# A chunked state-space scan feeding a GELU MLP on one core: weight quarters and B, C of unit 1 issued from ACT's queue

## The chip, the core and the metric

The kernel runs on one core of one Trainium2 chip. The core has five engines with an instruction queue each: PE (TensorE, matmul), DVE (VectorE), ACT (ScalarE), POOL (GpSimd) and SP (SyncE, which only issues transfers and waits). An engine works through its own queue in order; semaphores tell one engine that another, or a transfer, is done. The metric is the device time of one execution in microseconds (us), lower being better. Times in profile rows are counted from the start of the profiled span.

## The reference

Two stages follow each other. The first is a scan over 24 chunks of 32 positions for 4 batches and 8 heads; the second is an MLP over the 3072 resulting tokens.

```python
# x: 4 x 8 x 768 x 32, a: 4 x 8 x 768, B and C: 4 x 8 x 768 x 16, all float32
for c in range(nc):                      # chunks of 32
    cum = np.cumsum(log_a[chunk], -1)
    M = einsum('bhin,bhjn->bhij', Cc, Bc) * exp(cum_i - cum_j) * causal
    y = einsum('bhij,bhjd->bhid', M, xc) + einsum('bhin,bhnd->bhid', Cc, state) * exp(cum)
    state = exp(sum(la)) * state + sum_j(Bc_j * xc_j * exp(cum_last - cum_j))
t = y.transpose(0, 2, 1, 3).reshape(3072, 256)
h = t @ w_in                             # 256 x 2048
g = 0.5 * h * (1 + tanh(sqrt(2 / pi) * (h + 0.044715 * h**3)))
out = g @ w_out                          # 2048 x 256
```

## The kernel before

The kernel takes its own chunk length of 128 positions and treats two chunks (256 positions of one batch) as one unit, so there are 12 units, 0 to 11. For a unit the small loads are B and C (128 KB each, `load_bc`, line 163) and x (256 KB, `load_x`, line 171). The decays `a` are one load of 96 KB at the start (line 173). DVE scales B and C by decay factors (`f_mul`, line 338), PE or a transposing DMA turns them round (`f_T`, `f_XT`), DVE makes a masked copy `ce` (`f_F`; for unit 0 half of it is made on ACT, line 381), PE forms the Gram blocks `gb` (`f_G`), DVE masks them into `m` (`f_M`), PE adds up the result (`f_Y`) and ACT copies it as bf16 into `xm` (`f_yev`, line 250; for unit 0 DVE copies one half). The chain of states (`f_D`, `f_S`, `f_SP`) goes from chunk to chunk. The chunk decays `pend` come from one small matmul (`f_pp`), which in this kernel is written into bank GB[1], the bank of the Gram blocks.

The MLP works on the same 256 tokens as a unit: 8 pieces of four matmuls with `w_in` (`f_s1`, line 511), each followed by a GELU on ACT (`f_gelu`, line 519), and for each 128 tokens 16 matmuls with `w_out` (`f_s2`, line 528), an evacuation (`f_oev`) and a store. Both weights are 2 MB in float32, loaded in four quarters of 512 KB each (`load_wi`, line 242, and `load_wo`, line 246, into tiles `wf`) and cast to bf16 (`f_wi`, `f_wo`, lines 250 and 252).

The order of everything is planned by a list scheduler, `run_order` (line 33): each piece of work is a node with an engine, an estimated duration, a priority and dependencies, and the nodes are then emitted engine by engine in that order. In the plan all loads are one serial resource "DMA" in the order of the list `HEAD` (line 555). On the chip all of them except B of unit 0 are issued by SP, one after the other: a, C0, x0, wi0, C1, wi1, B1, x1, wi2, wi3, C2, wo0, B2, wo1, wo2, wo3, x2, C3, and so on (the digit is the unit or the quarter). PE runs matmuls without a use (line 788) in planned gaps of the first 20 us.

In the built program eight semaphores serve all loads of SP and ACT, given out in turn in program order; the issue of a load first waits for the landing of the load that had its semaphore before, eight loads earlier.

Of the kernel before, what the change touches and what calls it, by code (L numbers as in the profile page):

```python
# [109 lines left out]
def kernel(  # L110
# [10 lines left out]
    nc = tc.nc  # L121
# [13 lines left out]

    const = ctx.enter_context(tc.tile_pool(name="const", bufs=1))
    ldn = ctx.enter_context(tc.tile_pool(name="ldn", bufs=NP))
    wfp = ctx.enter_context(tc.tile_pool(name="wfp", bufs=6))
    ldx = ctx.enter_context(tc.tile_pool(name="ldx", bufs=NP))
    xpool = ctx.enter_context(tc.tile_pool(name="xpool", bufs=4))  # L140
    WB = 4
# [79 lines left out]
    rps = {}  # L221
# [17 lines left out]

    def load_wi(q):  # L240
        WF[("i", q)] = wfp.tile([128, 2, 512], FP32, name="wf")
        nc.sync.dma_start(out=WF[("i", q)], in_=wi[:, :, q * 512:(q + 1) * 512])  # L242

    def load_wo(q):
        WF[("o", q)] = wfp.tile([128, 4, d_model], FP32, name="wf")
        nc.sync.dma_start(out=WF[("o", q)], in_=wo[:, 4 * q:4 * q + 4])

    def copy(eng, o, i):
        if eng == "ACT":
# [6 lines left out]
    def f_wi(q, k0, k1, eng):  # L256
        copy(eng, w_in_sb[:, k0:k1, q * 512:(q + 1) * 512], WF[("i", q)][:, k0:k1])

    def f_wo(q, eng):
        copy(eng, w_out_sb[:, 4 * q:4 * q + 4], WF[("o", q)])  # L260


    def f_clip():
# [276 lines left out]
    def f_store(gc, q):  # L540
# [31 lines left out]
    def frees(n, *by, i=0):  # L572
        if n.alloc:
            n.frees[i] += list(by)


    nload = [0]
    T0 = 0.95

    def none():  # L580
        pass

    def load_act(dur, k, fn, *args):
        i = add("ACT", 0.55, fn, *args, nc.scalar, deps=[agate], prio=k[0])
        return load(dur, none, deps=[i])

    def load(dur, fn, *args, deps=(), alloc=()):
        nload[0] += 1
        return add("DMA", DF * dur, fn, *args, deps=deps, done=1.35, alloc=alloc, prio=nload[0])
# [6 lines left out]
    agate = add("ACT", 2.8, none, prio=-300)  # L596
    an = load(T0 + 0.3, none)
    an.done = 1.55
    bl[0, 1] = bl[0, 0] = load(2 * LB, none)

    def load_x_n(j):
        xl[j] = load_act(LX, AQ["x", j], load_x, j) if ("x", j) in AQ else load(LX, load_x, j, nc.sync)

    def load_b_n(j, i):
        a = ("bc"[i], j)
        bl[j, i] = load_act(LB, AQ[a], load_bc, j, i) if a in AQ else load(LB, load_bc, j, i, nc.sync)

    def load_w_n(k, q):
        (win_l, won_l)[k][q] = load((LI, LO)[k], (load_wi, load_wo)[k], q, alloc="wf")

    for kind, i in HEAD:
        {"x": load_x_n, "b": lambda j: load_b_n(j, 0), "c": lambda j: load_b_n(j, 1),
         "wi": lambda q: load_w_n(0, q), "wo": lambda q: load_w_n(1, q)}[kind](i)
    for j in range(T3, NP):
        load_b_n(j, 1)
        load_b_n(j, 0)
# [2 lines left out]
    for q in range(4):  # L619
        e = WENG[0][q].split("+")  # L620
        wi_n[q] = [add(f, wdur[f] / len(e) + 0.03 * (len(e) - 1), f_wi, q, k * 2 // len(e),
                       (k + 1) * 2 // len(e), f, deps=[win_l[q]], prio=-8 + q) for k, f in enumerate(e)]
        e = WENG[1][q]
        wo_n[q] = add(e, wdur[e], f_wo, q, e, deps=[won_l[q]], prio=20 + q)
        frees(win_l[q], *wi_n[q])
        frees(won_l[q], wo_n[q])


    cl = add("DVE", 0.55, f_clip, deps=[an], prio=-190)
# [9 lines left out]
    ppn = add("PE", 0.3, f_pp, deps=[pen, RT0], prio=-100)  # L639
    pendn = add("ACT", 0.22, f_pend, deps=[ppn], prio=-66)  # L640
    RTN = add("PE", 0.9, f_RTN, deps=[ppn], prio=RP, alloc="bk")
    rnn = [add("ACT", 0.28, f_rn, r, deps=[RTN], prio=5) for r in range(2)]
    frees(RTN, *rnn)
# [5 lines left out]
    for j in range(NP):  # L649
# [3 lines left out]
        if b and t == 0:  # L653
# [4 lines left out]
                     deps=[bl[j, i], *hold, pnn[b] if b else rlo if not i else rc1 if j else rc0, *gone(j)])  # L658
              for i in (1, 0)}
        bnn[j] = ml[0]  # L660
        if j == 0:
# [27 lines left out]
        xcn[j] = add("POOL", 0.66, f_castx, j, "POOL", deps=[xl[j], pgate, *gone(j)],  # L689
                     prio=10.0 * g0 - 10 if j else -96)  # L690
        u = j
        q = 10.0 * g0
        nd = kept(u)
        if u == 2:
            RTN.deps.append(Yn[1])
        if u <= MERGE:
            Gn[u] = add("PE", 0.37, f_G, u, prio=(-85, -50)[u] if u < 2 else q, deps=Fn[u] + Mn.get(u - 1, []))
# [28 lines left out]
        full = MERGE <= u < NP - 1  # L726
        Yn[u] = add("PE", 0.42 + 0.11 * sum(gc % CPB > 0 for gc in (g0, g0 + 1)) + (0.5 if full else 0.0),
# [26 lines left out]
    for g, (c0, n) in enumerate(GROUPS):  # L754
        per = 512 // (n * Q)
        for tt in range(n):
            gc = c0 + tt
            for q in range(4):
                need = [geln[(g, i)] for i in range(4 * n) if i * per <= 4 * q + 3]
                nd = add("PE", 0.437, f_s2, g, tt, q, deps=need[-1:] + [wo_n[q], prev],  # L760
                         prio=PB + 10 * c0 + 10 * n + 2.5 * (4 * tt + q) + 1.2, alloc="bk" if q == 0 else ())
                if q == 0:
                    first = nd
                prev = nd
# [5 lines left out]
            else:  # L770
                add("OUT", 0.05, f_store, gc, nc.sync, deps=[oevn[gc]], prio=gc)

    Dns[1].deps.append(gpn[(0, 3)])
    for n, u in later:
        n.deps.append(gpn[(u, 0)])

# [12 lines left out]
                                 start=True, stop=True)  # L789
        return fill  # L790

    pools = {"bk": 4, "gram": 1, "m": 2, "wf": 6}
    for t, fn in run_order(nodes, pools, idle=idle, wait=("DVE", "POOL")):
        fn()

# [29 lines left out]
```

## Time and profile before

| what | value |
|---|---|
| median of 3 runs | 118.8 us (118.76 to 119.0) |
| the profiled execution, its time | 119.01 us |
| its span, first to last instruction | 117.3 us |
| PE busy | 108.0 us (92%) |
| ACT, DVE, POOL busy | 72.1, 60.9, 31.0 us |
| granted PE clock | 1.000 |
| read from HBM, written | 10.58 MB, 3.15 MB |

Span and time of the profiled execution differ by 1.7 us of start and end outside the span. Busy PE is modelled from pipelined matmuls, so it says where PE had work, not that it worked at its peak. A row of the timeline gives the start, the duration, engine, line, operation, tiles and count of a run of equal instructions, and in brackets how long the engine sat idle before and what ended that. "SPq" and "ACTq" are the sequencers of these engines when they issue a transfer.

### The profile page before, as it was taken

The numbers are of one execution on the slowest core, as the hardware profiler recorded it, in microseconds if no ns is written. First come the engines' busy times: TensorE is split into PE (matmuls) and PEld (weight loads), VectorE is DVE, ScalarE is ACT, GpSimd is POOL, SyncE is SP. The second block draws the span as 40 slices with busy tenths as digits, with TensorE's granted clock in tenths as the row PEclk, the third lists the DMA queues.
The fourth block names the chain that finished last, engine by engine and source line by source line (L and its number), as shares of the span: only waits on it lengthen the run. The fifth ranks groups of instructions, "written<-read, shape, count | busy, mean of one in ns | idle before, by whom it ended". The sixth has DMA issues, their size and how long they took to land.

```text
span 117.3 us, 3834 instructions
## 1 busy us (share of the span) xinstructions
PE 108.0 (92%) x1638; PEld 91.7 (78%) x1638; DVE 60.9 (52%) x130; ACT 72.1 (61%) x156; POOL 31.0 (26%) x57
## 2 busy tenths in 40 slices
PE   5985767998999999999999999999999999999980
PEld 5863546787888888888888888888888888888860
DVE  2876685493687396671892943905708309000110
ACT  5063866773449559495685683783965866857610
POOL 6964364455332214103401303102111010000000
PEclk9999999999999999999999999999999999999999
DMA  3989999999979796499942962141101111011031
GB/s 74 209 245 221 263 253 293 347 169 184 222 150 157 128 229 164 75 225 188 144 78 56 215 164 62 45 50 45 50 0 45 50 38 52 6 45 48 0 98 45
DMA packets 46850, 15.04 MB, mean 128 GB/s; under 512 B 42320, under 2 KB 45232, under 8 KB 46832
## 3 DMA queue, kind: packets, MB, share of 16 engines
q1 hardware_dynamic: 44928, 12.29, 51.2%
q0 software_dynamic: 864, 2.36, 6.9%
q8 instruction: 13, 0.21, 0.8%
q10 hardware_dynamic: 1040, 0.13, 0.7%
q14 instruction: 5, 0.04, 0.1%
HBM read 10.58 MB, written 3.15 MB: 117 GB/s over the span
## 4 chain that ended last, share of the span: by engine, by line
PE 74%; DMA 11%; SPq 8%; POOL 2%; issue 1%; DVE 0%; DVEq 0%
PE bk L528 36%; PE bk L511 30%; DMA wf<-in_moe_w_out_dram 6%; DMA wf<-in_moe_w_in_dram 5%; SPq L242 5%; PE bk L434 3%; PE gb L399 3%; SPq L171 2%; PE bk L423 2%; PE bk L449 1%; SPq L163 1%; POOL w_out_sb L252 1%; POOL w_in_sb L252 1%; DVE o_sb L537 0%; SPq L173 0%
## 5 line engine op out<-in xcount | busy, mean ns | idle before, releaser
L519 ACT ACTIVATE gT<-bk 128x512 bf16<-128x512 f32 x96 | 50.6, 601 | 10.6 <-PE bk L511 10.6
L528 PE MATMUL bk<-w_out_sb,gT 128*128 128x256 bf16 x384 | 49.1, 273 | 0.9 <-POOL w_out_sb L252 0.5
L511 PE MATMUL bk<-xm,w_in_sb 128*128 128x256 bf16 x384 | 47.5, 273 | 1.2 <-POOL w_in_sb L252 1.1
L528 PEld LDWEIGHTS <-gT 128*128 128x128 bf16 x384 | 36.6, 98 | 7.4 <-issue 3.2
L511 PEld LDWEIGHTS <-w_in_sb 128*128 128x128 bf16 x384 | 37.2, 98 | 6.3 <-POOL w_in_sb L252 1.7
L409 DVE TENSOR_TENSOR m<-gb,tri 128x1024 bf16<-128x1024 f32 x23 | 27.8, 1217 | 1.7 <-PE gb L399 1.7
L542 POOL DMA_DIRECT2D out_dram<-o_sb x18 | 9.9, 551 | 42.5 <-ACT o_sb L535 40.6
L535 ACT ACTIVATE o_sb<-bk 128x256 f32<-128x256 f32 x22 | 8.5, 387 | 11.7 <-ACT xm L250 5.1
L477 DVE SCALAR_TENSOR_TENSOR s_new<-s_new,pend,bk 128x64 f32<-128x64 f32 x16 | 4.4, 275 | 19.1 <-ACT xm L250 18.4
L250 ACT ACTIVATE xm<-bk 128x256 bf16<-128x256 f32 x23 | 7.6, 380 | 9.5 <-PE bk L449 8.4
L338 DVE TENSOR_TENSOR bc<-bc,fac 128x256 bf16<-128x256 f32 x24 | 9.6, 430 | 5.6 <-DMA bc<-in_B_dram 3.3
L252 POOL CAST x<-x_t 128x512 bf16<-128x512 f32 x12 | 7.5, 629 | 12.1 <-DMA x_t<-in_x_dram 11.7
L493 DVE SCALAR_TENSOR_TENSOR sp_new<-s_new,pend,bmask 128x256 bf16<-128x256 f32 x19 | 9.6, 534 | 0.1
L537 DVE COPY o_sb<-bk 128x256 f32<-128x256 f32 x2 | 0.8, 424 | 14.0 <-PE bk L528 14.0
L383 DVE TENSOR_SCALAR ce<-bt,par 128x256 bf16<-128x256 bf16 x22 | 5.9, 318 | 2.8 <-ACT bt L250 1.7
L788 PE MATMUL bk<-wz 128*128 128x128 bf16 x66 | 6.2, 261 | 1.3 <-DVE warm L180 1.3
L788 PEld LDWEIGHTS <-wz 128*128 128x128 bf16 x66 | 5.2, 121 | 1.6 <-DVE warm L180 1.2
L434 PE MATMUL bk<-m,x 64*32 64x128 bf16 x384 | 5.2, 219 | 0.7 <-DVE m L409 0.7
L252 POOL CAST w_out_sb<-wf 128x1024 bf16<-128x1024 f32 x4 | 4.2, 1040 | 4.8 <-DMA wf<-in_moe_w_out_dram 4.8
L399 PE MATMUL gb<-ce,bt 32*64 32x256 bf16 x192 | 5.3, 280 | 0.1
L252 POOL CAST w_in_sb<-wf 128x1024 bf16<-128x1024 f32 (+1 forms) x4 | 3.7, 932 | 4.4 <-DMA wf<-in_moe_w_in_dram 4.4
L475 DVE COPY s_new<-bk 128x64 f32<-128x64 f32 x3 | 0.7, 224 | 7.5 <-ACT xm L250 7.5
(61 smaller groups left out, 45.7 us busy)
## 6 DMA issues: line engine op xcount, KB each, us to landing
x_t<-in_x_dram SPq DMA_DIRECT2D x12, 256.0 KB, 4.6
out_dram<-o_sb POOLq DMA_DIRECT2D x18, 128.0 KB, 3.0
wf<-in_moe_w_in_dram SPq DMA_DIRECT2D x4, 512.0 KB, 6.1
wf<-in_moe_w_out_dram SPq DMA_DIRECT2D x4, 512.0 KB, 7.5
bc<-in_C_dram SPq DMA_DIRECT2D x12, 128.0 KB, 4.5
bc<-in_B_dram SPq DMA_DIRECT2D x11, 128.0 KB, 4.2
out_dram<-o_sb SPq DMA_DIRECT2D x6, 128.0 KB, 1.7
bc<-in_B_dram ACTq DMA_DIRECT2D x1, 128.0 KB, 3.1
```

Of the source, the lines that this page charges most:

```text
L252: nc.gpsimd.tensor_copy(out=o, in_=i)
L338: nc.vector.tensor_tensor(out=d["bc16"][:, i], in0=d["bc"][:, i].rearrange("p h (r n) -> p r h n", r=2), in1=f.rearrange("p r (h o) -> p r ...
L399: nc.tensor.matmul(out=GB[g // 2][ks, g % 2, 256 * r:256 * r + 256], lhsT=d["bt"][gs, 0, r, ks], rhs=ce[gs, :, :, ks], start=True, stop=Tr ...
L409: nc.vector.tensor_tensor(out=state[("m", u, f)].rearrange("p g r e t -> p g (r e t)"), in0=state.pop(("gc", u, f), gram[f]).rearrange("p ...
L434: nc.tensor.matmul(out=y[k][32 * q:32 * q + 32, w * Q:(w + 1) * Q], lhsT=X16[u][ks, r, 32 * h:32 * h + 32], rhs=m[w][ks, q // 2, r, q % 2, :],
L493: nc.vector.scalar_tensor_tensor(out=sp_new.rearrange("p (g d) -> p g d", g=4), in0=state[("s", gc)].rearrange("p (o d) -> p o d", o=1).to ...
L511: nc.tensor.matmul(out=hp[:, j * nt:(j + 1) * nt], lhsT=w_in_sb[:, kc, fi * 128:(fi + 1) * 128], rhs=xm[:, kc, c0 * Q:c0 * Q + nt], start= ...
L519: nc.scalar.activation(gts[g][:, i * per:(i + 1) * per, 0:nt], hps.pop((g, i)).rearrange("p (j t) -> p j t", j=per), AF.Gelu_apprx_tanh)
L528: nc.tensor.matmul(out=ops[gc], lhsT=gts[g][:, fi, tt * Q:(tt + 1) * Q], rhs=w_out_sb[:, fi, :], start=(fi == 0), stop=(fi == NF - 1), ski ...
L535: nc.scalar.activation(o_sb, ops.pop(gc), AF.Copy)
L542: q.dma_start(out=out[u * W:(u + 1) * W].rearrange("(p r) m -> r p m", r=2)[r], in_=ops.pop(gc))
L788: nc.tensor.matmul(out=BK[j][:, 0:128], lhsT=wz[:, 0:128], rhs=wz[:, 0:128], start=True, stop=True)
```

## The change

ACT's queue now issues B0 (as before), C1, B1 and all eight weight quarters; SP keeps a, C0, x0, x1, C2, B2, x2, C3, B3, x3 and the rest. The tiles `wf` go from 6 buffers to 8. `f_pp` gets a bank of its own from the pool of four. The cast of wi0 is split in two halves on POOL, its half on ACT for wi1 goes to POOL, and the casts of wo2 and wo3 are split between POOL and DVE. Unit 2's transposed copy is made on DVE in place of ACT. D and G of unit 3 stand by themselves (`MERGE` 3). The planner gets new durations, a limit on outstanding descriptors (`RING`), a second load resource "DW" for the weights, priorities `WP` for the weight issues on ACT and two dependencies for them (wi2 after `f_rlo`, wo0 after the copy `s0`).

```diff
-    wfp = ctx.enter_context(tc.tile_pool(name="wfp", bufs=6))
+    wfp = ctx.enter_context(tc.tile_pool(name="wfp", bufs=8))
...
     load_bc(0, 0, nc.scalar)
     load_bc(0, 1, nc.sync)
+    load_bc(1, 1, nc.scalar)
+    load_bc(1, 0, nc.scalar)
...
-        nc.sync.dma_start(out=WF[("i", q)], in_=wi[:, :, q * 512:(q + 1) * 512])
+        nc.scalar.dma_start(out=WF[("i", q)], in_=wi[:, :, q * 512:(q + 1) * 512])
...
-        nc.sync.dma_start(out=WF[("o", q)], in_=wo[:, 4 * q:4 * q + 4])
+        nc.scalar.dma_start(out=WF[("o", q)], in_=wo[:, 4 * q:4 * q + 4])
...
-    def f_wo(q, eng):
-        copy(eng, w_out_sb[:, 4 * q:4 * q + 4], WF[("o", q)])
+    def f_wo(q, k0, k1, eng):
+        copy(eng, w_out_sb[:, 4 * q + 2 * k0:4 * q + 2 * k1], WF[("o", q)][:, 2 * k0:2 * k1])
...
-    def f_pp():
-        rps["pp"] = GB[1][:, 0, 0:NCH]
+    def f_pp(bk):
+        rps["pp"] = bk[:, 0:NCH]
...
+    WP = (-185, -184.9, -179.5, -179.4, -64, -63, -59, -58)
...
-    MERGE = 2
+    MERGE = 3
...
-    DF = 1.07
+    DF = 1.0
+    RING = 212
...
-    PET = {0: "ACT", 1: "ACT", 2: "ACT", 3: "ACT"}
-    LB, LX, LI, LO, XD, XL = 0.85, 1.15, 1.6, 1.5, 0.6, 3.6
-    HEAD = [("x", 0), ("wi", 0), ("c", 1), ("wi", 1), ("b", 1), ("x", 1), ("wi", 2), ("wi", 3),
-            ("c", 2), ("wo", 0), ("b", 2), ("wo", 1), ("wo", 2), ("wo", 3), ("x", 2)]
-    WENG = [("POOL", "POOL+ACT", "POOL", "POOL"), ("POOL", "POOL", "POOL", "POOL")]
+    PET = {0: "ACT", 1: "ACT", 2: "DVE", 3: "ACT"}
+    LB, LX, LI, LO, XD, XL = 0.92, 1.25, 1.85, 1.65, 0.6, 3.6
+    HEAD = [("x", 0, 2.6), ("x", 1, 3.0), ("c", 2, 5.5), ("b", 2, 3.7), ("x", 2, 2.3)]
+    SIDE = [*(("wi", q, 1.6, WP[q]) for q in range(4)), *(("wo", q, 1.75, WP[4 + q]) for q in range(4))]
+    WENG = [("POOL+POOL", "POOL", "POOL", "POOL"), ("POOL", "POOL", "POOL+DVE", "POOL+DVE")]
...
-    RP = 2000
+    RP = 4
+    XP = {0: -96, 1: -9}
+    D1 = None
+    WD = 0
...
+    was, issue = agate, {}
+    for i, dur in ((1, 5.0), (0, 1.6)):
+        bl[1, i] = add("DW", dur, none, done=1.35, prio=-i)
+    for k, (kind, i, dur, prio) in enumerate(SIDE):
+        was = issue[kind, i] = add("ACT", 0.5, load_wi if kind == "wi" else load_wo, i, deps=[was],
+                                   prio=prio)
+        lat = add(f"L{k}", 1.1, none, deps=[was])
+        n = add("DW", dur, none, deps=[lat], done=1.35, prio=k)
+        (win_l, won_l)[kind == "wo"][i] = n
...
+    issue["wi", 2].deps.append(rlo)
...
+                if WD is not None:
+                    issue["wo", WD].deps.append(sn)
...
-    Dns[1].deps.append(gpn[(0, 3)])
+    if D1 is not None:
+        Dns[1].deps.append(gpn[(0, D1)])
```

In the built program ACT's queue begins as follows. The names are those of the loads above; behind an issue stands the landing for which it waits because of the semaphores given out in turn, two queues now sharing the eight. The planner has no node for these waits.

| ACT's queue in order | waits for |
|---|---|
| issue B0, C1, B1 | nothing |
| load of the function table, `warm` | DVE's `warm` |
| issue wi0 | nothing |
| issue wi1 | landing of C0 |
| `fac` (`f_rlo`) | DVE |
| issue wi2 | landing of wi0 |
| issue wi3 | landing of B2 |
| `ce` of unit 0, `bt`, `pend`, `gs`, `s0`, `s_new` | PE, DVE |
| issue wo0 | landing of x3 |
| issue wo1 | landing of wi2 |
| issue wo2 | landing of C4 |
| issue wo3 | landing of wi3 |
| `xm` of unit 0, `bt` of unit 1, GELUs of group 0 | PE, DVE |

SP's queue is a, C0, x0, x1, C2 (waits for B0), B2 (a), x2 (C1), C3 (x0), B3 (B1), x3 (x1), C4 (C2), B4 (wi1), x4 (x2), C5 (C3), B5 (B3), and then the first transposing DMA.

More of the change, by code (lines that the diff above doesn't have):

```diff
@@ L577, with load @@
     nload = [0]
-    T0 = 0.95
+    T0 = 1.05
     def none():
         pass
[L583 to L587, printed above, removed]
+    ring = []
+    def load(dur, fn, *args, deps=(), alloc=(), desc=65):
         nload[0] += 1
-        return add("DMA", DF * dur, fn, *args, deps=deps, done=1.35, alloc=alloc, prio=nload[0])
+        cum = (ring[-1][1] if ring else 0) + desc
+        full = [m for m, c in ring if cum - c <= RING]
+        room = [add(f"R{nload[0]}", 1.1, none, deps=full[:1])] if cum > RING and full else []
+        n = add("DMA", DF * dur, fn, *args, deps=[*deps, *room], done=1.35, alloc=alloc, prio=nload[0])
+        ring.append((n, cum))
+        return n
     win_l, won_l, wi_n, wo_n = {}, {}, {}, {}
@@ L594, with load_x_n, load_b_n @@
     Gn, Mn, Yn, yevn, Sn, SPn, Fn, bnn, gcn, Dns = ({} for _ in range(10))
-    agate = add("ACT", 2.8, none, prio=-300)
-    an = load(T0 + 0.3, none)
+    agate = add("ACT", 3.8, none, prio=-300)
+    an = load(T0 + 0.3, none, desc=7)
     an.done = 1.55
     bl[0, 1] = bl[0, 0] = load(2 * LB, none)
[L601 to L613, printed above, removed]
+    def load_x_n(j, dur=None):
+        xl[j] = load(dur or LX, load_x, j, nc.sync)
+    def load_b_n(j, i, dur=None):
+        bl[j, i] = load(dur or LB, load_bc, j, i, nc.sync)
+    for kind, i, dur in HEAD:
+        if kind == "x":
+            load_x_n(i, dur)
+        else:
+            load_b_n(i, "bc".index(kind), dur)
+    was, issue = agate, {}
[7 more added lines that the diff above has]
+        (win_l, won_l)[kind == "wo"][i] = n
     for j in range(T3, NP):
@@ L622 @@
                        (k + 1) * 2 // len(e), f, deps=[win_l[q]], prio=-8 + q) for k, f in enumerate(e)]
[L623 to L626, printed above, removed]
+        e = WENG[1][q].split("+")
+        wo_n[q] = [add(f, wdur[f] / len(e) + 0.03 * (len(e) - 1), f_wo, q, k * 2 // len(e),
+                       (k + 1) * 2 // len(e), f, deps=[won_l[q]], prio=20 + q) for k, f in enumerate(e)]
     cl = add("DVE", 0.55, f_clip, deps=[an], prio=-190)
@@ L637 @@
     rlo = add("ACT", 0.2, f_rlo, deps=[RT0, rc0], prio=-180)
+    issue["wi", 2].deps.append(rlo)
     rc1 = add("DVE", 0.36, f_rc1, deps=[rc0, rlo], prio=-62)
-    ppn = add("PE", 0.3, f_pp, deps=[pen, RT0], prio=-100)
+    ppn = add("PE", 0.3, f_pp, deps=[pen, RT0], prio=-100, alloc="bk")
     pendn = add("ACT", 0.22, f_pend, deps=[ppn], prio=-66)
+    frees(ppn, pendn)
     RTN = add("PE", 0.9, f_RTN, deps=[ppn], prio=RP, alloc="bk")
@@ L660 @@
         bnn[j] = ml[0]
+        if j == 1:
+            ml[1].deps.append(Mn[0][1])
+            ml[0].deps.append(Mn[0][1])
         if j == 0:
@@ L689 @@
         xcn[j] = add("POOL", 0.66, f_castx, j, "POOL", deps=[xl[j], pgate, *gone(j)],
-                     prio=10.0 * g0 - 10 if j else -96)
+                     prio=XP.get(j, 10.0 * g0 - 10))
         u = j
@@ L696 @@
         if u <= MERGE:
-            Gn[u] = add("PE", 0.37, f_G, u, prio=(-85, -50)[u] if u < 2 else q, deps=Fn[u] + Mn.get(u - 1, []))
+            Gn[u] = add("PE", 0.37, f_G, u, prio=(-85, -62)[u] if u < 2 else q, deps=Fn[u] + Mn.get(u - 1, []))
             xd = add(f"X{u}", 0.8, none, deps=[xcn[u]]) if u else xcn[u]
@@ L759 @@
                 need = [geln[(g, i)] for i in range(4 * n) if i * per <= 4 * q + 3]
-                nd = add("PE", 0.437, f_s2, g, tt, q, deps=need[-1:] + [wo_n[q], prev],
+                nd = add("PE", 0.437, f_s2, g, tt, q, deps=need[-1:] + wo_n[q] + [prev],
                          prio=PB + 10 * c0 + 10 * n + 2.5 * (4 * tt + q) + 1.2, alloc="bk" if q == 0 else ())
@@ L790, in idle @@
         return fill
-    pools = {"bk": 4, "gram": 1, "m": 2, "wf": 6}
+    pools = {"bk": 4, "gram": 1, "m": 2}
     for t, fn in run_order(nodes, pools, idle=idle, wait=("DVE", "POOL")):
```

## The prediction

> **What bounds the kernel now.** I read the chain of waits first: it tells from where on PE alone sets the end.
>
> ```profile
> 25.69 1.05 POOL w_out_sb L252
> 26.74 0.04 issue
> 26.79 1.91 PE bk L528 x16
> ...
> 109.90 3.94 PE bk L528 x36
> ```
>
> Columns are start, duration, engine with what it writes, line and count. Up to 26.79 us the chain runs through weights (a load, then the cast at 25.69); from 26.79 to 113.84 (109.90 + 3.94) it is PE without a break, 87.05 us of it. So this change can win or lose only in the ramp before 26.79: a microsecond of PE work that the ramp loses comes back as a microsecond at the end. Next the ramp itself, from the first useful MLP matmul on, by windows: all of PE, then the useless matmuls of line 788 alone.
>
> ```profile
> 12.60:26.79 14.19, 11.98 (x175) 9.13 (x174) 9.36 (x16) 10.36 (x22) 6.86 (x7) 1.00 1.02 264
> 12.60:26.79 14.19, 0.56 (x4) 0.27 (x4) 1.00 1.02 264
> ```
>
> The second number is the length of the window, the third PE's busy time, the last the GB/s moved; the granted clock (1.00) is full. Useful work is 11.98 - 0.56 = 11.42 us, so PE is idle for useful ends 14.19 - 11.42 = 2.77 us after 12.60. That is all that earlier weights could win if unit 0 comes no earlier. From 12.60 on PE has 11.42 + 87.05 = 98.47 us of useful work. The forecast is then: new start of the MLP, plus 98.47, plus new idle time.
>
> What sets 12.60 is unit 0's way through ACT, and what the loads do meanwhile stands in the rows of the engines that wait for them.
>
> ```profile
> 0.80 0.44 ACTq L163 DMA_DIRECT2D bc<-in_B_dram  x1
> 1.28 1.28 ACT L181 ACT_TABLE_LOAD   x1 [1.28 <-PEq L809]
> 2.57 0.20 ACT L181 ACTIVATE warm<-warm 128x1 f32<-128x1 f32 x1
> 5.84 0.21 ACT L293 ACTIVATE fac<-gb 128x48 f32<-128x48 f32 x1 [3.06 <-DVE fac L287]
> 6.75 0.47 ACT L381 ACTIVATE ce<-bk,par 128x256 bf16<-128x256 bf16 x1 [0.71 <-PE bk L353]
> ...
> 9.05 0.22 ACT L474 ACTIVATE s_new<-bk 128x64 f32<-128x64 f32 x1
> 11.29 0.63 ACT L250 ACTIVATE w_in_sb<-wf 128x512 bf16<-128x512 f32 x1 [2.02 <-DMA wf<-in_moe_w_in_dram]
> 11.83 0.36 ACT L250 ACTIVATE xm<-bk 128x256 bf16<-128x256 f32 x1
> 12.60 0.61 PE L511 MATMUL bk<-xm,w_in_sb 128*128 128x256 bf16 x4
> ```
>
> ACT needs 2.52 us from `ce` to the end of `s_new` (6.75 to 9.27); PE's first matmul of line 511 comes 0.77 us after ACT's `xm` begins. The table load starts right behind the issue on ACT's sequencer: the queue goes in order.
>
> ```profile
> 8.04 1.04 POOL L252 CAST w_in_sb<-wf 128x1024 bf16<-128x1024 f32 x1 [0.94 <-DMA wf<-in_moe_w_in_dram]
> ...
> 13.24 0.61 POOL L252 CAST x<-x_t 128x512 bf16<-128x512 f32 x1 [1.31 <-DMA x_t<-in_x_dram]
> 14.59 1.04 POOL L252 CAST w_in_sb<-wf 128x1024 bf16<-128x1024 f32 x1 [0.74 <-DMA wf<-in_moe_w_in_dram]
> 16.78 1.04 POOL L252 CAST w_in_sb<-wf 128x1024 bf16<-128x1024 f32 x1 [1.15 <-DMA wf<-in_moe_w_in_dram]
> 19.57 1.04 POOL L252 CAST w_out_sb<-wf 128x1024 bf16<-128x1024 f32 x1 [1.75 <-DMA wf<-in_moe_w_out_dram]
> 21.81 1.04 POOL L252 CAST w_out_sb<-wf 128x1024 bf16<-128x1024 f32 x1 [1.19 <-DMA wf<-in_moe_w_out_dram]
> 11.73 0.48 DVE L338 TENSOR_TENSOR bc<-bc,fac 128x256 bf16<-128x256 f32 x1 [0.64 <-DMA bc<-in_B_dram]
> ...
> 17.88 0.42 DVE L338 TENSOR_TENSOR bc<-bc,fac 128x256 bf16<-128x256 f32 x1 [0.68 <-DMA bc<-in_C_dram]
> ...
> 20.29 0.60 DVE L338 TENSOR_TENSOR bc<-bc,fac 128x256 bf16<-128x256 f32 x1 [1.00 <-DMA bc<-in_B_dram]
> wf<-in_moe_w_in_dram SPq DMA_DIRECT2D x4, 512.0 KB, 6.1
> wf<-in_moe_w_out_dram SPq DMA_DIRECT2D x4, 512.0 KB, 7.5
> bc<-in_C_dram SPq DMA_DIRECT2D x12, 128.0 KB, 4.5
> ```
>
> Each of these waits ended with a landing, so with SP's order they are a clock of bytes (a is 96 KB, an x 256 KB): 1,120 KB had landed when wi0 did (8.04), 1,888 with B1 (11.73), 2,144 with x1 (13.24), 2,656 with wi2 (14.59), 3,168 with wi3 (16.78), 3,296 with C2 (17.88), 3,808 with wo0 (19.57), 3,936 with B2 (20.29), 4,448 with wo1 (21.81). The transfers are the scarce thing of the ramp, 264 GB/s in the window above.
>
> **The change part by part.** *Weight issues on ACT.* Eight issues at the 0.58 us of an unhindered one, and C1 and B1 at 0.44:
>
> ```profile
> 2.35 1.83 SPq L242 DMA_DIRECT2D wf<-in_moe_w_in_dram  x1
> 4.23 0.47 SPq L163 DMA_DIRECT2D bc<-in_C_dram  x1
> 4.75 0.58 SPq L242 DMA_DIRECT2D wf<-in_moe_w_in_dram  x1
> ```
>
> C1, B1, wi0 and wi1 fall into ACT's idle time before 5.84 and cost nothing; without that cover they would be 2.0 us. (The row at 2.35 shows that an issue can also take 1.83 us; that bound makes the table load late, and wi0 with it.) The other issues are not free, because of what they wait for. wi2 waits for wi0, wi3 for B2, wo0 for x3, wo2 for C4 and wo3 for wi3, and behind these stand `ce` and, after wo3, `xm` of unit 0. That a transfer's wait holds the later issues of its queue is seen on SP now:
>
> ```profile
> SPq L348 <- DVE bc L338: 15.9, 5, 5.4
> ```
>
> Five transposing transfers held SP for 15.9 us in all, up to 5.4 us each. No issue before waits for a landing noticeably, since in one queue the load eight places back is always in; with two queues of unlike pace it is not. The Trainium skill, "DMA: Bandwidth & Descriptors", section "Anatomy of one DMA", says the same in general: the wait of a transfer happens on the issuing sequencer before dispatch, the transfer engines do not wait. By that rule the sum below holds as it stands; were the wait in the transfer engine, ACT would go on and the time would be the one of the faster rival.
>
> *First wait, wi3 for B2.* Before B2 are in the queues a, B0, C0, C1, B1, C2, x0, x1, and on ACT's wi0 and, right behind it, wi1: with B2 2,400 KB. By the clock of bytes that is 13.9 us. The ends: without wi1 1,888 KB, 11.7; with wi2 too 2,912 KB, 15.7. I take 13.9, as wi1 is issued long before. With the issue ACT goes on at 14.5 instead of 6.75, and `s_new` ends 2.52 later, at 17.0.
>
> *Second wait, wo0 for x3.* SP has by then moved a and all of units 0 to 3 (2,144 KB), ACT four quarters (2,048 KB): 4,192 KB. The clock of bytes gives 21.05. The lower end leaves out wi3 (3,680 KB, 19.1). For the upper end: 768 KB more of these bytes are small loads than in the same sum of before, and small loads are slower:
>
> ```profile
> 2.00:4.00 2.00, 2.00 (x21) 2.00 (x20) 0.93 (x2) 0.76 (x2) 1.79 (x5) 1.00 1.20 203
> 20.00:22.00 2.00, 1.56 (x17) 1.29 (x17) 0.60 (x1) 1.13 (x5) 0.81 (x2) 1.00 1.08 344
> 28.00:30.00 2.00, 2.00 (x28) 1.61 (x26) 1.17 (x3) 0.56 (x2) 1.35 (x2) 1.00 1.21 193
> ```
>
> 0.79 MB at 200 in place of 344 GB/s is 1.6 us more, 22.6. I take 21.3, near the middle row. It is later than 17.0, so this wait decides. Then come four issues, 4 x 0.58 = 2.3 (C4, 128 KB at 200 GB/s, is 0.65 behind x3 and so in; wi3 too), then `xm` 0.36 and a step of 0.1: PE starts the MLP at 24.1, 11.5 us later than 12.60. The ends are 21.9 and 26.5 (the upper one with 1.1 for issues that find the queue full, near the 1.83 row). These rows also speak to a rule against the change: two queues together moved 203 GB/s (2 to 4 us), one alone 193 (28 to 30). The Trainium skill, "DMA: Bandwidth & Descriptors", section "Issuing engines are not separate DMA queues", says that issuing from several engines saves issue time only, as all share the same 16 DMA engines. The trace agrees; by the rule the gain without waits would be at most that issue time, by the rows the 2.77 us of idle.
>
> *Idle time after the new start.* At 24.1 all of `w_in` is there, and `w_out`, issued at 21.3 to 23.6, follows within a few us, so PE's waits for casts of before mostly fall away; unit 1's way through `bt`, Gram, mask and state remains, behind the first eight GELUs. Bounds 0.5 and 2.77 us; I take 1.0, near the lower end, since weights were the chain before. *Bank for `f_pp`, split casts, unit 2's copy on DVE, unit 3 unmerged, more buffers.* None adds a load or a large instruction. The bank lets the Gram blocks start without `pend`, a gain under 0.2 us; the half casts on DVE (0.61 on POOL for that size, as on x at 13.24) and DVE's copy in place of ACT's lie beside ACT's GELUs; if that cover is gone they cost at most 0.6 each. Together 0, from -0.2 to +1.2.
>
> **The sum** against the profiled execution: PE ends at 24.1 + 98.47 + 1.0 = 123.6 instead of 113.84, 9.7 later: 119.01 + 9.7 = 128.7. The median lies 0.2 below the profiled execution's time: 118.8 + 9.7 = 128.5.
>
> **The rivals.** *Small loads first.* If SP's small loads outrun the weights, or B1's issue is held like the row at 2.35, wi0 lands late and wi2's wait decides: after 2,144 KB at 200 GB/s from 2 us (13.0) come four quarters at 344 (6.1) with wi2's issue and wi3's each behind a landing, some 2 us, then 2.5 of unit 0 and the four issues 2.3: about 26, PE at 26.4, time 118.8 + 13.8 - 1.8 = 130.8. For it speaks that small loads were never held by weights for long so far; against it that there was one queue only.
>
> *Only the first wait.* If small loads run far ahead yet weights do too, x3, C4 and wi3 are in when ACT is through at 17.0; then the four issues and `xm`: PE at 19.8, 7.2 later, less 1.8: 124.2. Against it: 4,192 KB by 17.0 us would need more than the trace's rate.
>
> *Faster.* If the waits find their loads landed (B2 and x3 soon, since SP now has no weights in its queue), ACT runs as before, PE starts at 12.6 and the weights, without issue jams, cut the idle 2.77 to about 1.0: 117.0. For it: SP's 1.83 us jam goes. Against: the same bytes must pass before B2, whatever the queue, and at 6.75 not even the 1,120 KB through wi0 had landed.
>
> *No change.* wi3 and the wo are late by as much as the earlier casts win: 118.8. It needs two unlike sums to meet.
>
> **How the numbers follow.** Two waits as summed 0.62, small loads first 0.14, only the first wait 0.11, faster 0.10, no change 0.03. Predicted: 128.5. The likeliest case alone, with start ends 21.9 and 26.5 and idle ends: 125.5 to 133. Down to the one-wait case with its start a little earlier, and up to 133, the range is 121.5 to 133, leaving out the faster and unchanged cases. About 0.2% (0.24 us) is what this measurement can tell from no change: faster 0.10, same 0.03, slower 0.87.
>
> **What would show it.** ACT's rows: `ce` of unit 0 near 14.5 instead of 6.75, issues on ACT's sequencer with long gaps before them; `xm` of unit 0 near 23.7; first matmul of line 511 near 24.1; PE then almost without gaps. `ce` before 8 would refute the first wait, `xm` within 3 us of `s_new` the second. If PE's first MLP matmul is at 13 and its end is early, the waits do not hold ACT and the prediction is wrong in its core.

## The result, and the profile after

The changed kernel takes 130.6 us (median of 4 runs, 129.66 to 131.41) against 118.78 us for the kernel before (4 runs, 118.58 to 119.0). The ratio is 1.099, its 95% interval 1.092 to 1.107: slower, by some 11.8 us. The profiled execution took 130.71 us with a span of 129.0.

Line numbers of the changed kernel are two higher than before for `xm` (L252), `ce` (L383) and the first MLP matmul (L513). First its page, in extract:

```profile
PE 111.9 (87%) x1639; PEld 95.0 (74%) x1639; DVE 61.7 (48%) x133; ACT 71.8 (56%) x154; POOL 31.8 (25%) x58
...
PEclk9999999558999999999999999999999999999999
...
q1 hardware_dynamic: 39648, 7.84, 34.8%
q10 hardware_dynamic: 6320, 4.59, 13.0%
...
PE 78%; DMA 10%; SPq 7%; ACTq 2%; issue 0%; DVE 0%; ACT 0%; DVEq 0%
```

ACT's busy time is what it was (72.1 before). PE's busy time grew from 108.0 to 111.9 us, its idle time in the span from 9.3 to 17.1. ACT's queue (q10) now moves 4.59 MB, as the change wants. The last row is the split of the chain that ended last: 10% of the span are transfers and 7% SP's sequencer, ahead of PE. The next view shows that chain in order of time (start, duration, what):

```profile
13.29 8.87 DMA x_t<-in_x_dram
22.16 0.02 issue
22.18 0.45 ACTq L248
...
23.90 0.59 ACTq L248
24.50 0.05 issue
24.55 0.39 ACT xm L252
24.94 0.04 issue
24.98 2.72 PE bk L513 x12
```

This part of the chain runs from the transfer of x3 through ACT's four `w_out` issues to `xm` of unit 0 and the first MLP matmul. Unit 0 needs neither x3 nor `w_out` at that point. ACT's own timeline (start, duration, engine and line, operation, count, and in brackets the idle time before it and what ended it):

```profile
3.05 1.28 ACT L183 ACT_TABLE_LOAD   x1 [3.05 <-issue]
...
6.11 0.21 ACT L295 ACTIVATE fac<-gb 128x48 f32<-128x48 f32 x1 [1.56 <-DVE fac L289]
10.73 3.44 ACTq L244 DMA_DIRECT2D wf<-in_moe_w_in_dram  x2
14.21 0.47 ACT L383 ACTIVATE ce<-bk,par 128x256 bf16<-128x256 bf16 x1 [7.89 <-DMA bc<-in_B_dram]
...
16.60 0.23 ACT L476 ACTIVATE s_new<-bk 128x64 f32<-128x64 f32 x1
22.18 2.32 ACTq L248 DMA_DIRECT2D wf<-in_moe_w_out_dram  x4
24.55 0.38 ACT L252 ACTIVATE xm<-bk 128x256 bf16<-128x256 f32 x1 [7.72 <-issue]
```

Before, `ce` stood at 6.75 and `xm` at 11.83. Now ACT waits 7.89 us ahead of `ce`, ended by a landing of a B, and 7.72 us ahead of `xm`, most of it ahead of the first `w_out` issue at 22.18. The 7.89 us hold two waits: wi2 could be issued only at 10.73, when wi0 landed (issued at 3.12, 7.6 us to landing), and wi3 only at 13.8, when B2 landed (issued at 5.54, 8.2 us to landing). The same on PE:

```profile
14.74 0.65 PE L401 MATMUL gb<-ce,bt 32*64 32x256 bf16 x16 [6.96 <-ACT ce L383]
...
24.98 2.72 PE L513 MATMUL bk<-xm,w_in_sb 128*128 128x256 bf16 x12 [4.88 <-ACT xm L252]
...
31.30 0.39 PE L425 MATMUL bk<-bt,sp_new 128*128 128x128 bf16 x4
...
121.19 4.09 PE L530 MATMUL bk<-w_out_sb,gT 128*128 128x256 bf16 x36
```

The MLP starts at 24.98 instead of 12.60, 12.38 later, and PE ends at 125.28 instead of 113.84, 11.4 later. From the new start to the end it takes 100.3 us, 1.83 more than the 98.47 of useful work counted before.

### The profile page after: what moved, and what is told of

It is laid out like the page before. It is cut to its first block, busy times and chain, and to the rows that moved or that the text cites. A ratio compares the mean times of both kernels' runs of the same rounds, so it can differ in the third digit from the quotient of the medians.

```text
span 129.0 us, 3835 instructions
## 1 busy us (share of the span) xinstructions
PE 111.9 (87%) x1639; PEld 95.0 (74%) x1639; DVE 61.7 (48%) x133; ACT 71.8 (56%) x154; POOL 31.8 (25%) x58
## 3 DMA queue, kind: packets, MB, share of 16 engines
q10 hardware_dynamic: 6320, 4.59, 13.0%
q0 software_dynamic: 864, 2.36, 5.5%
## 4 chain that ended last, share of the span: by engine, by line
PE 78%; DMA 10%; SPq 7%; ACTq 2%; issue 0%; DVE 0%; ACT 0%; DVEq 0%
PE bk L513 34%; PE bk L530 33%; DMA x_t<-in_x_dram 7%; SPq L163 5%; PE gb L401 3%; PE bk L436 3%; DMA bc<-in_B_dram 3%; SPq L171 2%; ACTq L248 2%; PE bk L425 2%; PE bk L451 1%; PE bk L275 0%; PE bk L361 0%; DVE o_sb L539 0%; ACT xm L252 0%
## 5 line engine op out<-in xcount | busy, mean ns | idle before, releaser
L521 ACT ACTIVATE gT<-bk 128x512 bf16<-128x512 f32 x96 | 51.7, 598 | 13.8 <-PE bk L513 13.5
L513 PE MATMUL bk<-xm,w_in_sb 128*128 128x256 bf16 x384 | 50.6, 280 | 4.9 <-ACT xm L252 4.9
L530 PE MATMUL bk<-w_out_sb,gT 128*128 128x256 bf16 x384 | 50.4, 273 | 0.0
L513 PEld LDWEIGHTS <-w_in_sb 128*128 128x128 bf16 x384 | 38.2, 100 | 10.7 <-issue 5.4
L252 ACT ACTIVATE xm<-bk 128x256 bf16<-128x256 f32 x23 | 7.6, 381 | 17.8 <-PE bk L451 8.8
L340 DVE TENSOR_TENSOR bc<-bc,fac 128x256 bf16<-128x256 f32 x24 | 10.7, 489 | 0.1
L812 PE MATMUL bk<-wz 128*128 128x128 bf16 x67 | 7.6, 301 | 1.3 <-DVE warm L182 1.3
L401 PEld LDWEIGHTS <-bt 32*64 32x64 bf16 x192 | 2.1, 108 | 8.1 <-issue 7.6
L812 PEld LDWEIGHTS <-wz 128*128 128x128 bf16 x67 | 6.9, 145 | 1.4 <-DVE warm L182 1.2
L385 DVE TENSOR_SCALAR ce<-bt,par 128x256 bf16<-128x256 bf16 x22 | 5.0, 271 | 6.1 <-ACT bt L252 6.0
L254 POOL CAST w_out_sb<-wf 128x1024 bf16<-128x1024 f32 (+1 forms) x4 | 3.3, 826 | 7.3 <-DMA wf<-in_moe_w_out_dram 7.3
L383 ACT ACTIVATE ce<-bk,par 128x256 bf16<-128x256 bf16 x1 | 0.5, 473 | 7.9 <-DMA bc<-in_B_dram 7.9
```

The source lines that it names most:

```text
L254: nc.gpsimd.tensor_copy(out=o, in_=i)
L340: nc.vector.tensor_tensor(out=d["bc16"][:, i], in0=d["bc"][:, i].rearrange("p h (r n) -> p r h n", r=2), in1=f.rearrange("p r (h o) -> p r ...
L401: nc.tensor.matmul(out=GB[g // 2][ks, g % 2, 256 * r:256 * r + 256], lhsT=d["bt"][gs, 0, r, ks], rhs=ce[gs, :, :, ks], start=True, stop=Tr ...
L513: nc.tensor.matmul(out=hp[:, j * nt:(j + 1) * nt], lhsT=w_in_sb[:, kc, fi * 128:(fi + 1) * 128], rhs=xm[:, kc, c0 * Q:c0 * Q + nt], start= ...
L521: nc.scalar.activation(gts[g][:, i * per:(i + 1) * per, 0:nt], hps.pop((g, i)).rearrange("p (j t) -> p j t", j=per), AF.Gelu_apprx_tanh)
L530: nc.tensor.matmul(out=ops[gc], lhsT=gts[g][:, fi, tt * Q:(tt + 1) * Q], rhs=w_out_sb[:, fi, :], start=(fi == 0), stop=(fi == NF - 1), ski ...
```

## The experiments

The runs below were made in three later sets on three chips, where the kernel before took 118.6 to 119.9 us (medians of the sets); so ratios are compared, and positions in the profiles. In the first set the kernel before scattered from 118.27 to 122.55 us. Against only those of its executions that took under 120 us, the four ratios of that set (1.0145, 1.0155, 1.0086 and 1.038 below) would be 1.020, 1.024, 1.010 and 1.044, so half a per cent between them says nothing. No kernel leaves out work; some add instructions without a use, which is said there.

**All loads back on SP.** Two words of the changed kernel; B1 and C1 stay on ACT, and so do all its other parts.

```diff
-        nc.scalar.dma_start(out=WF[("i", q)], ...
+        nc.sync.dma_start(out=WF[("i", q)], ...
-        nc.scalar.dma_start(out=WF[("o", q)], ...
+        nc.sync.dma_start(out=WF[("o", q)], ...
```

> The changed kernel with its eight weight issues back on SP's queue (C1 and B1 stay on ACT), all else as changed. If the waits of ACT's weight issues for landings cost the 11.8 us: ACT's ce of unit 0 comes near 6.8 us instead of 14.2, the first matmul of line 513 at 12.5 to 14 instead of 25.0, and the time is 117.5 to 119.5 us. If the newly planned order, the split casts or the bank cost it: 125 us or more, with the MLP still starting after 18 us.

Measured: ratio 1.0145 (1.0041 to 1.0249). `ce` is at 6.69 and `xm` at 11.31, as before, and the first MLP matmul at 13.90. The time, 121.59 us, is over the 117.5 to 119.5 expected. So most of the loss of 9.9% comes with the two lines that move the weight issues; the bank, the casts, the priorities and the rest cost some 1.5% here, 0.4 to 2.5 by the interval.

**Only `w_out` back on SP.**

> Only the four wo issues go back to SP; wi0 to wi3 stay on ACT, and with fewer loads between them they now wait for nothing, a, C0 and C1. Waits: ce near 6.8, MLP from 12.5 to 14 us, 117 to 120 us. If the wi issues on ACT themselves cost it: ce after 10 us and 122 us or more.

Measured: ratio 1.0155 (1.003 to 1.028), `ce` at 6.67, `xm` at 11.37, first MLP matmul at 12.06; the time, 121.93 us, is over the 117 to 120 expected. This moved the places in the program, so the three `w_in` issues that wait also waited for early loads, a, C0 and C1; no long wait is left on ACT. A new one showed up on PE (its timeline, same columns):

```profile
12.06 1.13 PE L513 MATMUL bk<-xm,w_in_sb 128*128 128x256 bf16 x8
...
24.07 0.40 PE L361 MATMUL bk<-ident,bc 128*128 128x128 bf16 x4 [2.69 <-DVE bc L340]
```

DVE had waited 5.36 us for B2, which stands behind all four `w_out` loads in SP's queue here.

**All eight on ACT, other pairs.** The runs so far change the queue and the waits together. This one keeps every weight issue on ACT and changes which landing each waits for: two writes of one column by ACT, into the tiles of C2 and of x2, move these loads to a later place in the program, so that the eight semaphores meet in other pairs.

```diff
             d["bc"] = ldn.tile([128, 2, H, 2 * N], FP32, name="bc")
+            if j == 2:
+                nc.scalar.activation(d["bc"][:, i, 0, 0:1], warm, AF.Copy)
...
         nc.scalar.dma_start(out=WF[("o", q)], in_=wo[:, 4 * q:4 * q + 4])
+        if q == 3:
+            XF[2] = ldx.tile([128, H, 2 * D], FP32, name="x_t")
+            nc.scalar.activation(XF[2][:, 0, 0:1], warm, AF.Copy)
```

In the built program wi1 to wi3 then wait for B0, a and C0, and the four `w_out` for x0, x1, wi0 and wi1: nothing later than the second quarter of `w_in`.

> All eight weight issues stay on ACT, with the same bytes. Two tiny ACT copies write one column of the tiles of C2 and of x2 before these are loaded, so SP's loads come later in the program and the semaphores pair otherwise: wi1 waits for B0, wi2 for a, wi3 for C0, wo0 for x0, wo1 for x1, wo2 for wi0, wo3 for wi1. If the pairing of waits costs the time: ce near 6.8 us, the first MLP matmul at 12.5 to 14, 116.5 to 119.5 us. If issuing weights from ACT or two queues sharing the transfers cost it: 125 us or more.

Measured: ratio 1.0086 (1.0036 to 1.0136). The MLP starts at 14.84 and the time is 120.33 us, both a little over what was expected. ACT's timeline, and then the chain that ended last:

```profile
6.72 0.47 ACT L390 ACTIVATE ce<-bk,par 128x256 bf16<-128x256 bf16 x1 [0.74 <-PE bk L362]
...
14.42 0.37 ACT L259 ACTIVATE xm<-bk 128x256 bf16<-128x256 f32 x1
```

```profile
4.41 7.46 DMA wf<-in_moe_w_in_dram
11.87 0.04 issue
11.91 2.36 ACTq L251
14.27 0.05 issue
14.31 0.20 ACT x_t L254
```

With the same queue and the same bytes, 9 of the 9.9% are gone: `ce` is where it was before, and the last landing ahead of `xm` is wi1 at 11.87 in place of x3 at 22.16. What stays is that landing and one issue that takes 2.36 us by itself, against 0.58 for an unhindered one; `xm` stands 2.6 us later than before for the two. The pairs are not all that changed, though: SP's loads of C2 and x2 must now wait for ACT's two writes, and all that stands behind them in SP's queue waits too. C2 and B2 are issued at 8.92 and 9.34, in the changed kernel at 4.20 and 5.54, so the first weights had fewer small loads beside them.

```profile
8.92 0.37 SPq L165 DMA_DIRECT2D bc<-in_C_dram  x1
9.34 0.58 SPq L165 DMA_DIRECT2D bc<-in_B_dram  x1
```

**One write less, in two ways.** With the write into C2 alone, the last three `w_out` wait for wi0, wi2 and the landing of the first `w_out`; the first wait is gone and a long second one stays.

> As the variant with two tiny copies, but only the one for C2: wi1 to wi3 wait for B0, a and C0, while wo1 waits for wi0, wo2 for wi2 and wo3 for the landing of wo0. Waits: ce near 6.8 us (the first wait is gone), but xm of unit 0 stands behind wo0's landing, issued near 10 and landing near 17, so the MLP starts at 17 to 19 us and the time is 121 to 124.5 us. If only the first wait mattered: 117 to 119.5 us.

Measured: ratio 1.038 (1.028 to 1.048), `ce` at 7.26, first MLP matmul at 19.27, somewhat later than the 17 to 19 expected; the time, 124.38 us, is inside the range. The row of `xm`:

```profile
18.84 0.38 ACT L254 ACTIVATE xm<-bk 128x256 bf16<-128x256 f32 x1 [8.84 <-DMA wf<-in_moe_w_out_dram]
```

With the write into x2 alone the latest landing for which ACT waits is that of wi0.

> Of the two small ACT writes only the one on x of unit 2 stays, so that x2 is issued behind the w_out quarters. With this, wi1 waits for C0, wi2 for C1, wi3 for x0, wo0 for B1, wo1 for x1, wo2 for wi0, wo3 for C2, none of them a late landing. Theory of the waits: ce of unit 0 by 8 us (14.2 in the changed kernel), first MLP matmul between 12.5 and 16, time 118.5 to 121.5, ratio 1.00 to 1.02, although every weight quarter is still on ACT's queue and one instruction of 0.2 us is all that was added. Rival, the weights on ACT's queue are late by themselves because of the traffic of the small loads beside them: first MLP matmul after 18, ratio over 1.04.

Measured: ratio 1.0122 (1.0063 to 1.0181), `xm` at 15.31, first MLP matmul at 15.73; the chain has wi0 landing at 10.71 and two issues of 2.03 and 2.36 us behind it. One instruction of 0.20 us takes away seven eighths of the loss (9.9 to 1.2%). This is the cleaner test of the pairs: up to 7.6 us SP issues the same loads as in the changed kernel, within 0.05 us of the same times, and wi0 lands at 10.7 in both, yet `ce` runs at 7.63 in place of 14.21. Behind that, x2 and all later loads of SP stand until 19.11 here: x2 waits for ACT's write, and then still for B2, which landed only at 19.1. So the first wait is shown to come from the pairs alone; that the two long issues ahead of `xm` would take no longer with the small loads beside them is not shown. Over the three kernels and the changed one the MLP starts late where the landing that ends the waits is late: 14.84 and 15.73 with wi1 or wi0 in by 12 us, 19.27 with the first `w_out` at 18.81, 24.98 with x3 at 22.16.

**A late ACT without any queue.** If the waits matter only because ACT is late with unit 0, the kernel before must lose the same when ACT is made late by work of its own. In the kernel before, ACT writes a tile without a use, 19 or 10 times ahead of `xm` of unit 0, or 12 times ahead of `ce`:

```diff
     def f_yev(u, k, eng):
+        if u == 0 and eng == "ACT":
+            for _ in range(19):
+                nc.scalar.activation(junk, wz, AF.Copy)
```

> The kernel before, with all its loads on SP, and 19 writes without a use (128x512, some 0.6 us each) on ACT right ahead of its copy xm of unit 0: ACT is late there by some 11.4 us as it is in the changed kernel, but by work of its own and not by a queue. Theory that a late ACT at this place is all that the changed kernel lost: first MLP matmul at 23.5 to 24.5 (12.60 before), time longer by 9 to 12 us, ratio 1.075 to 1.10. Rival, the changed kernel lost its time in the memory traffic or in the casts and a late ACT alone is caught up in PE's idle stretches: ratio under 1.06.

> The same with 10 such writes, about 6 us. If every us of a late start costs nearly one us: first MLP matmul at 18 to 19, time longer by 3.5 to 6 us, ratio 1.03 to 1.05. Rival, there is slack of several us in the ramp: ratio under 1.02.

> The kernel before with 12 such writes, about 7.2 us, ahead of ACT's ce of unit 0 alone, so that ce runs at 13.5 to 14.5 as in the changed kernel, and nothing delays xm but the work behind ce. This is the first of the two waits by itself: first MLP matmul at 17.5 to 20, ratio 1.035 to 1.055 (the rival of the prediction in which only the first wait decides had 124.2 us). If the first wait were what cost the changed kernel its time, the ratio would be over 1.08; if it is hidden, under 1.02.

Measured: 1.0987 (1.0933 to 1.104) with 19, 1.0524 (1.0471 to 1.0577) with 10, 1.0577 (1.0505 to 1.0649) ahead of `ce`. The first is as large as the loss of the changed kernel, and inside its range. The other two came out a little over what was expected: the writes take 0.66 us each and not 0.6, and behind a late `ce` the MLP starts at 20.44, later than the 20 foretold. PE's rows with 19 writes:

```profile
24.68 2.72 PE L515 MATMUL bk<-xm,w_in_sb 128*128 128x256 bf16 x12 [11.34 <-ACT xm L251]
...
121.69 4.09 PE L532 MATMUL bk<-w_out_sb,gT 128*128 128x256 bf16 x36
```

| kernel | `ce` | first MLP matmul | PE's end | from one to the other |
|---|---|---|---|---|
| before | 6.75 | 12.60 | 113.83 | 101.2 |
| before, 10 writes ahead of `xm` | 6.73 | 18.30 | 119.44 | 101.1 |
| before, 12 writes ahead of `ce` | 14.02 | 20.44 | 121.10 | 100.7 |
| before, 19 writes ahead of `xm` | 7.79 | 24.68 | 125.78 | 101.1 |
| changed | 14.21 | 24.98 | 125.28 | 100.3 |
| changed, two small writes | 6.72 | 14.84 | 114.71 | 99.9 |
| changed, write into C2 alone | 7.26 | 19.27 | 119.05 | 99.8 |
| changed, write into x2 alone | 7.63 | 15.73 | 115.31 | 99.6 |
| changed, all loads on SP | 6.69 | 13.90 | 115.10 | 101.2 |
| changed, `w_out` on SP | 6.67 | 12.06 | 117.15 | 105.1 |

In the kernel before, each microsecond by which the MLP starts later comes back as one at the end: from 12.60 to 24.68 is 12.08 us, from 113.83 to 125.78 is 11.95. PE's idle time of the ramp catches up next to nothing of it. The start is not always the whole story: with `w_out` on SP the MLP starts earliest of all, and PE loses 4 us behind it, 2.69 of them in the wait for B2.

**Is it PE's clock?** In the changed kernel the first 12 MLP matmuls take 2.72 us, against 1.49 before, at a granted clock of 0.50. The row of before:

```profile
12.60 1.49 PE L511 MATMUL bk<-xm,w_in_sb 128*128 128x256 bf16 x12
```

So 42 matmuls without a use were put into PE's idle stretch of the changed kernel, and 22 into that of the version with the two small writes.

```diff
+        if g == 0 and i == 0:
+            for _ in range(42):
+                nc.tensor.matmul(out=GB[0][:, 0, 0:128], lhsT=wz[:, 0:128], rhs=wz[:, 0:128],
+                                 start=True, stop=True)
```

> The changed kernel with 42 more matmuls without a use (128x128, into GB[0]) on PE right before the first MLP matmul, that is in PE's idle stretch from 20.1 to 24.98 us; nothing else. Waits and slow PE clock theory: the first MLP matmul stays at 25.0 (24.8 to 25.3), but the granted clock of PE does not fall to 0.50 behind it: the first 12 MLP matmuls take 1.5 us (2.72 in the changed kernel), the first 32 some 2 to 3 us less, and the time falls by 1 to 2.5 us, to a ratio of 1.08 to 1.09. Rival, the casts of w_out or the GELUs set the pace behind the late start: the first 12 matmuls are faster but the time stays within 0.4 us of the changed kernel, 1.095 to 1.105. Second rival, the clock falls whatever PE does: share 0.50 is again in the record and nothing changes.

> The version with the two small ACT writes that change the pairing (all eight weight loads on ACT, first MLP matmul at 14.84), plus 22 matmuls without a use on PE in its idle stretch from 12.3 to 14.8 us. Slow clock theory: no share of 0.50 from 15.1 to 18.5, the first 12 MLP matmuls take 1.5 us instead of 2.47, the ratio to the kernel before falls from 1.009 to 0.995 to 1.002. Rival, what is left over the kernel before is the start of the MLP at 14.84 against 12.60 and the evenness of the rest: the ratio stays at 1.005 to 1.012.

Measured: 1.090 (1.083 to 1.097) and 1.0111 (1.0041 to 1.018; it rests on three of six executions, the other three took 121.9 to 122.3 us). In the first the clock fell in spite of the matmuls; in the second it stayed full, as foretold, but the ratio is in the range of the rival. The first, on PE:

```profile
19.81 2.52 PE L512 MATMUL gb<-wz 128*128 128x128 bf16 x42
24.71 2.36 PE L517 MATMUL bk<-xm,w_in_sb 128*128 128x256 bf16 x12 [2.38 <-ACT xm L252]
...
30.39 0.39 PE L425 MATMUL bk<-bt,sp_new 128*128 128x128 bf16 x4
```

The 42 ran at full clock and were through at 22.3, 2.4 us too early, and the clock fell all the same, if for less long. The stretch from the first MLP matmul to unit 1's state took 5.68 us (24.71 to 30.39) against 6.32 in the changed kernel (24.98 to 31.30), 0.64 less, and from the start to PE's end it took 99.66 instead of 100.3, again 0.64 less. In these two profiles, then, what the slow clock takes in this stretch comes back in full at the end; the interval of the ratio overlaps that of the changed kernel and doesn't settle it by itself. The second, on PE:

```profile
14.36 1.47 PE L524 MATMUL bk<-xm,w_in_sb 128*128 128x256 bf16 x12
15.82 0.42 PE L408 MATMUL gb<-ce,bt 32*64 32x256 bf16 x16
...
18.54 0.39 PE L432 MATMUL bk<-bt,sp_new 128*128 128x128 bf16 x4
...
23.84 0.40 PE L368 MATMUL bk<-ident,bc 128*128 128x128 bf16 x4 [2.62 <-DVE bc L347]
```

Here the clock stayed full and the same stretch took 4.18 us, but PE then stood 2.62 us before unit 2, whose B2 was issued at 10.10 and landed only at 23.36. At full clock PE only came to the next late load sooner, and the time did not fall. In that version, then, the slow clock is for the most part hidden by B2 (without the 22 matmuls B2 was in at 22.76, and unit 2 began at 23.24 in place of 23.84); in the changed kernel, where B2 is in by 13.8, it is not.

**Towards a version that beats both.** `w_out` on SP and B2 ahead of it, in two ways: by the planner, which moves much else too, and by hand; both edits in extract.

```diff
-                    issue["wo", WD].deps.append(sn)
+                    issue["wo", WD].deps.extend([sn, bl[2, 0], xl[2]])
```

> w_in on ACT as in the change, w_out on SP but planned behind B2 and x2 (in the run with w_out on SP, B2 stood behind the four w_out loads, and PE was idle from 21.4 to 24.07 for it). Theory that this late B2 was what that run lost: no idle of PE over 1 us between 20 and 26, first MLP matmul at 12 to 13, ratio 0.99 to 1.005. Rival: w_out now comes late in its place and PE waits for a w_out cast between 20 and 30, ratio 1.01 to 1.03.

Measured: ratio 1.0671 (1.0609 to 1.0733), far over what was expected, and the mechanism of the change once more. The new order gave wi2 the pair x1 and wi3 the pair wi0:

```profile
9.02 1.97 ACTq L244 DMA_DIRECT2D wf<-in_moe_w_in_dram  x2
11.04 0.47 ACT L383 ACTIVATE ce<-bk,par 128x256 bf16<-128x256 bf16 x1 [4.93 <-DMA wf<-in_moe_w_in_dram]
```

By hand, with all `w_out` on SP, `load_wo(0)` issues B2 first, and wi1 to wi3 wait for C0, C1 and x0:

```diff
     def load_wo(q):
+        if q == 0:
+            load_bc(2, 0, nc.sync)
```

> The change with w_out on SP and B of unit 2 issued ahead of the four w_out loads; with it wi1 waits for C0, wi2 for a load 8 places before it that lands early, C1, wi3 for x0; w_out waits for C1's and x1's neighbours and wi0, none late. If the late B2 was all that the run with w_out on SP lost (PE idle 2.69 us at 24.07): no idle of PE over 1 us between 20 and 26, first MLP matmul at 12 to 14, ratio 0.99 to 1.005. Rival: the slow PE clock or the w_in casts keep it at 1.01 to 1.02.

Measured: ratio 1.0077 (1.0038 to 1.0116, 12 executions), first MLP matmul at 13.38, no idle of PE over 0.2 us from 20 to 26. The idle time before B2 is gone, and yet the ratio is just over the 0.99 to 1.005 expected: the kernel is still not faster than the one before. No version tried here beats it. What makes up the last 0.8 to 1.5% of these versions was not taken apart: a start of the MLP up to 3 us later, waits for `w_in` casts and slow stretches of PE's clock stand in one or another of their profiles.

## Why the prediction was right

The forecast was 128.5 us, 121.5 to 133; measured 130.6. Step by step:

- *The mechanism.* Two waits on ACT's queue, as summed; the second sets the start. Both stand in the trace, the small writes that change the pairs take nine tenths of the loss away (with SP's small loads held back too; the one write into x2 shows the first wait by itself), and a late ACT alone makes a loss of the same size in the kernel before (1.0987 against 1.0992).
- *First wait.* `ce` forecast at 14.5, measured 14.21, ended by a B as said; `s_new` forecast to end at 17.0, measured 16.83. B2 was forecast to land at 13.9 and landed at 13.7. What the sum left out is that wi2 waits for wi0, which landed at 10.7 here and at 8.04 before: ACT stood for it from 6.32 on. B2 came later still, so the sum did not suffer; where B2 is not in the way, that wait decides, as in the planner's version with `ce` at 11.04.
- *Second wait.* x3 forecast at 21.3, between 19.1 and 22.6; measured 22.16. That is toward the bound for slower small loads, and SP's issues of x2, C3 and x3 took 2.69, 2.22 and 2.75 us. The four issues took 2.32 (forecast 2.3), and the MLP started at 24.98 instead of 24.1. That the second wait decides and covers the first also held: with `ce` late alone the MLP starts at 20.44. The bounds 21.9 and 26.5 with idle times of 0.5 and 2.77 add up to 125.8 and 132.7, not quite the 125.5 and 133 given.
- *Idle time after the start.* Forecast 1.0, between 0.5 and 2.77; measured 1.83, inside the bounds but by luck, since it is not idle time. The casts of `w_in` were indeed all in by then (POOL did them from 18.6 to 23.1), and by the record PE is busy without a gap from 24.98 on. So the waits counted in the forecast are gone; in their place came PE's half clock, which the forecast had no term for. The stretch that took 6.32 us took 4.18 in the version whose clock stayed full, 2.1 less; all of the 1.83 can be that. This and the 0.9 of x3 are the terms that were mis-sized: 0.9 + 0.8 are the 1.7 us by which PE ends later than the forecast 123.6.
- *The small edits at nothing.* Bounds -0.2 to +1.2 us; with all loads on SP they and the new order of the loads cost 0.4 to 2.5%, 0.5 to 3 us. Whether one of them, or the order alone, costs it was not tried, nor whether it is paid in the changed kernel too, where the waits can cover it.
- *The rivals.* "Only the first wait" (124.2): the kernel before with `ce` late alone has the ratio 1.0577, 125.6 us on the first set's 118.78, so its price was 1.4 too low, and it isn't what happened. "Small loads first" (130.8) is close to the time measured, but not to the trace: wi0 was late and held wi2, as this rival says, but `ce` was released by B2 and the MLP by x3, not by wi2 and four quarters behind it. "Faster" and "no change" fell with `ce` at 14.21.
- *The pages.* That a wait stands on the issuing sequencer (the Trainium skill, "DMA: Bandwidth & Descriptors", "Anatomy of one DMA", written for gpsimd's path) is what the rows of ACT show here, 7.89 us. That a second issuing engine brings no second set of transfer engines (same page, "Issuing engines are not separate DMA queues") fits the runs whose waits were short, though they don't test it by themselves: weights on ACT 1.0086, on SP 1.0145, neither under 1.

## What to carry to other kernels

Before loads are moved to the queue of an engine that also computes, write down for every issue which landing it waits for in the built program, and what stands behind it on that engine: semaphores given out in turn over two queues tie an issue to loads it has nothing to do with, and one instruction more or less can change all the pairs behind it. Where one engine sets the end from early on, the first instruction of its long run is the number to watch first, since each microsecond there was one microsecond of time here; the next is what the engine loses right behind it, as the version with `w_out` on SP shows. A delay put in by hand, of the size in doubt and at the place in doubt, is a cheap test of such a claim.

## What the hardware did that was not expected

PE's granted clock halves in or just behind an idle stretch and stays half for some us of work. Windows of 2 us of the changed kernel (length, PE's busy time, then the granted clock, DMA share, GB/s):

```profile
20.00:22.00 2.00, 0.10 (x16) 1.00 0.64 97
22.00:24.00 2.00, 0.00 (x0) 0.73 0.93 187
24.00:26.00 2.00, 1.02 (x6) 0.50 0.98 248
26.00:28.00 2.00, 2.00 (x24) 0.50 1.03 300
28.00:30.00 2.00, 2.00 (x26) 0.57 1.13 338
30.00:32.00 2.00, 2.00 (x52) 1.00 0.73 230
```

PE goes idle at 20.1, the clock falls about 2.8 us later and is full again some 4.7 us after work has begun. The Trainium skill, "TensorE: Matmul & The Clock Gate", section "Part 1: The HAM clock gate", gives windows of 3.4 us for both steps; the trace agrees only roughly. Gaps shorter than that were enough: with the 42 matmuls PE was idle for 2.4 us (22.33 to 24.71), and the clock fell at 25.1, when work was already under way again, and was half until 28.5.

```profile
25.00:25.10 0.10, 0.10 (x3) 1.00 0.99 278
25.10:25.20 0.10, 0.10 (x2) 0.64 1.06 343
25.20:25.30 0.10, 0.10 (x2) 0.50 0.95 293
```

In the version with the two small writes a gap of 2.6 us did the same (half from 15.1 to 18.6). The page also warns of the record itself, and rightly: in the kernel with 12 writes ahead of `ce` the record says 1.00 throughout, yet its first 12 MLP matmuls take 2.77 us, as those at 0.50 do.

```profile
20.44 2.77 PE L514 MATMUL bk<-xm,w_in_sb 128*128 128x256 bf16 x12
```

The first row of windows shows another thing: in the last 2 us of ACT's wait for x3 the transfers moved 97 GB/s, against 293 from 18 to 20, while all four quarters of `w_out` stood unissued behind that wait.
